# Performer attention with two mixture layers: half tiles of keys of two head pairs in one tile, half tiles of queries of two batches in another, and the low parts of x last in the first layer's sums

## The chip, the cores and the metric

One core of a Trainium2 chip runs the whole program. The metric is the device time of one execution in microseconds (us). The engines are TensorE (PE in the profile; PEld is its load of the stationary operand), VectorE (DVE), ScalarE (ACT), GpSimd (POOL) and SyncE (SP), whose queue issues most DMA transfers.

## The reference

Three layers follow each other. The first is attention with exponential random features, the second a gated feed-forward layer, the third a mixture of eight experts with fixed capacity.

```python
# q, k, v: (4 batches, 8 heads, 576 rows, 64); omega: (128, 64)
def phi(x):
    proj = np.einsum('bhsd,md->bhsm', x, omega)
    h = proj - np.sum(x * x, axis=-1, keepdims=True) / 2.0
    h = h - np.max(h, axis=-1, keepdims=True)
    return np.exp(h) / np.sqrt(m)
q_p, k_p = (phi(q * scale), phi(k * scale))
kv = np.einsum('bhsm,bhsd->bhmd', k_p, v)
z = np.sum(k_p, axis=2)
num = np.einsum('bhsm,bhmd->bhsd', q_p, kv)
den = np.einsum('bhsm,bhm->bhs', q_p, z)[..., None] + 1e-06
# x = num / den as (2304 tokens, 512)
xn = x / rms * rms_g
g = xn @ w_gate
x = (g * sigmoid(g) * (xn @ w_val)) @ w_out          # 512 -> 1536 -> 512
logits = x @ moe2_w_gate                              # greedy: best logits first, 288 tokens per expert
out[mask] = np.maximum(x[mask] @ w1[e], 0.0) @ w2[e]  # for each expert e, 512 -> 1024 -> 512
```

## The kernel before

The attention is cut into **items**, and the items run through a software pipeline of **ticks**: in tick t item t is at lag 0, item t-1 at lag 1, and so on to lag 5. TensorE's order is the order of the code in `run_tick`; the other engines' order is chosen by the scheduler, with the attention at higher priority.

- A **key item** (`KItem(b, p, g)`) is batch b, head pair p, and up to two tiles of 128 keys (g = 0, 1, 2). A batch has 576 keys, four and a half tiles; the fifth is padded with zeros, so the item with g = 2 is short: one tile, half of it padding. At lag 0 a tile and `om` give the features of two heads (`pp`; three matmuls in high and low parts, or one in full precision, L391, for batch 0); VectorE takes the maximum (`mx`, L395), ScalarE the exponentials (`ft`, L398). At lag 1 the features times the values with a column of ones (65 columns a head, L432) are summed in a PSUM tile `pm` over the three items of the pair and copied to `kvs`.
- A **query item** (`QItem(b, t, hf)`) is one tile of 128 queries and four of the eight heads. The tiles of a batch are four whole ones and one of 64 rows, which is computed as a whole one. Lag 0 is as for keys; at lag 1 the features are transposed (L474) and copied (`qp`); at lag 2 they are multiplied with `kvs` (65 columns a head, L478) and VectorE divides (`dn`, L498 to L500); at lags 3 to 5 a tile is normed (`xn`), transposed (L483) and split into `xh` (high part) and `xl` (low part) of a block of 512 tokens.
- A batch has 12 key items and 10 query items, so there are 88 items and 93 ticks. Every float32 product in full precision shows as two records in the trace.
- When a block of 512 tokens is complete, its 24 **feed-forward steps** can run: 12 feature blocks f, for each the gate and the value product (`ffn_pe`, L614 to L616). One step is 12 matmuls of 512 tokens into `gv`, of which there are two; VectorE frees a `gv` with `th` (L626) or `hp` (L634, L638). A tick from `FFN_AT` (25) on holds one step, and a second one as long as weights remain to be converted.
- The weights come as 64-bit numbers. A **conversion** turns half a feature block into float32: ScalarE scales (L542), VectorE joins the words in three instructions (L546 to L548), ScalarE and GpSimd split high and low parts (L570, L571). A tick before `FFN_AT` starts half a conversion, a later one two, until the 24 of the gate and value weights are done. They are loaded to three buffers (`ws`) by SP's queue.

`pm` tiles come from three PSUM buffers, which keys (sums) and queries (transposes, products) share. What is left of the 120 steps when the attention ends runs in a loop behind it; then come the second product with the routing, and the experts.

## Time and profile before

| | |
|---|---|
| time, median of 3 runs | 948.57 us (948.55 to 948.75) |
| profiled execution, its own time | 950.67 us |
| its span | 948.9 us |
| TensorE busy | 924.3 us (97%) |
| VectorE busy | 530.2 us (56%) |
| ScalarE busy | 389.4 us (41%) |
| GpSimd busy | 226.2 us (24%) |
| granted TensorE clock, mean | 0.994 |

Busy time is a sum over stages that have different limits, and TensorE's is modelled at the end of each matmul; so a stage is read from its own stretch, and the price of an instruction of TensorE from the distance between two starts.

### The profile page before, as it was taken

Reading aid. Unit: us, or ns where it says so; the run is one execution under the profiler, and the core shown is the slowest. Engines: PE = TensorE matmul, PEld = TensorE weight load, DVE = VectorE, ACT = ScalarE, POOL = GpSimd, SP = SyncE. Lnnn points to the kernel's source line nnn. Section 1 sums busy time; section 2 is a strip of 40 time slices with the busy share of each in tenths; the row PEclk is TensorE's granted clock in tenths of the full one; section 3 lists DMA queues with packets and bytes.
Section 4 is the critical chain, followed back from the end, with each engine's and each line's share of the span. In section 5 each row is a group of like instructions: output and inputs, shape, how many; then the busy total and the mean of one; then the engine's idle time right before and its main releaser. Section 6 shows DMA issues by size and latency. Waiting matters only on the chain.

```text
span 948.9 us, 16526 instructions
## 1 busy us (share of the span) xinstructions
PE 924.3 (97%) x6349; PEld 804.8 (85%) x6349; DVE 530.2 (56%) x1221; ACT 389.4 (41%) x899; POOL 226.2 (24%) x291
## 2 busy tenths in 40 slices
PE   9998899999999999999999999999999999999996
PEld 7786689988888888877789777777779999999996
DVE  4899946752444334442236476666664655566651
ACT  6976445654554445532234101001004444444451
POOL 1365411322333322443323000000011222222211
PEclk9999999999999999999999999999999999999999
DMA  8546653452222321445666466776632666666650
GB/s 292 178 153 213 210 180 118 152 199 79 78 80 85 104 77 57 167 178 182 207 181 236 140 191 197 221 210 198 189 107 77 192 191 188 211 187 190 188 169 26
DMA packets 117151, 153.67 MB, mean 162 GB/s; under 512 B 6224, under 2 KB 78544, under 8 KB 117072
## 3 DMA queue, kind: packets, MB, share of 16 engines
q1 hardware_dynamic: 111264, 138.32, 46.9%
q0 software_dynamic: 3072, 9.44, 3.3%
q10 hardware_dynamic: 2736, 4.85, 1.3%
q8 instruction: 50, 0.82, 0.4%
q14 instruction: 29, 0.24, 0.1%
HBM read 108.55 MB, written 44.04 MB: 161 GB/s over the span
## 4 chain that ended last, share of the span: by engine, by line
PE 82%; issue 7%; DVE 7%; POOL 1%; DMA 1%; ACT 1%; POOLq 0%; ACTq 0%; SPq 0%; DVEq 0%
PE py L920 15%; PE gv L614 10%; PE gv L616 9%; PE gv L615 9%; PE pm L478 3%; PE ph L1034 3%; PE ph L1031 3%; PE ph L1032 3%; PE pm L432 3%; PE py L1042 3%; PE py L1043 3%; PE py L1044 3%; PE cnt L179 2%; PE pm L474 2%; DVE dw L547 2%
## 5 line engine op out<-in xcount | busy, mean ns | idle before, releaser
L614 PE MATMUL gv<-xh,wc 128*128 128x512 f32 (+1 forms) x480 | 184.9, 385 | 9.1 <-DVE th L626 7.9
L615 PE MATMUL gv<-xl,wc 128*128 128x512 f32 (+1 forms) x480 | 178.3, 371 | 1.5 <-DVE xl L522 1.5
L616 PE MATMUL gv<-xh,wc 128*128 128x512 f32 (+1 forms) x480 | 178.6, 372 | 0.0
L920 PE MATMUL py<-wc,ht 128*128 128x512 f32 x648 | 167.3, 404 | 0.0
L920 PEld LDWEIGHTS py<-wc,ht 128*128 128x128 f32 x648 | 114.8, 189 | 19.0
L614 PEld LDWEIGHTS gv<-xh,wc 128*128 128x128 f32 x480 | 91.4, 190 | 26.6 <-DVE th L626 8.5
L615 PEld LDWEIGHTS gv<-xl,wc 128*128 128x128 f32 x480 | 91.6, 191 | 16.1 <-DVE xl L522 2.2
L616 PEld LDWEIGHTS gv<-xh,wc 128*128 128x128 f32 x480 | 91.1, 190 | 16.4
L398 ACT ACTIVATE ft<-pp,mx 128x128 f32<-128x128 f32 x320 | 92.3, 372 | 18.3 <-DVE mx L395 17.0
L641 POOL TENSOR_TENSOR hp<-th,hp 128x512 fp32r<-128x512 f32 (+1 forms) x48 | 57.8, 1204 | 141.9 <-ACT hp L640 123.9
L626 DVE SCALAR_TENSOR_TENSOR th<-th,gv 128x512 f32<-128x512 f32 (+1 forms) x60 | 37.8, 630 | 94.4 <-ACT th L625 94.3
L891 DVE TENSOR_TENSOR wc<-ws,wc 128x512 fp32r<-128x512 f32 x128 | 84.7, 682 | 0.0
L1042 PE MATMUL py<-ehh,wc 128*128 128x288 f32 x256 | 77.7, 304 | 0.0
L1043 PE MATMUL py<-ehl,wc 128*128 128x288 f32 x256 | 75.9, 297 | 0.0
L1044 PE MATMUL py<-ehh,wc 128*128 128x288 f32 x256 | 75.8, 296 | 0.0
L1031 PE MATMUL ph<-exh,wc 128*128 128x288 f32 x256 | 71.6, 302 | 0.0
L1032 PE MATMUL ph<-exh,wc 128*128 128x288 f32 x256 | 69.8, 295 | 0.0
L931 ACT COPY ys<-py 128x512 f32<-128x512 f32 x18 | 10.6, 588 | 144.2 <-PE py L920 103.3
L901 ACT CAST wc<-ws 128x1024 fp32r<-128x1024 f32 x64 | 66.9, 1046 | 2.4 <-ACT ys L931 2.4
L395 DVE TENSOR_REDUCE mx<-pp 128x4 f32<-128x512 f32 (+1 forms) x88 | 56.0, 636 | 16.7 <-PE pp L388 9.3
L625 ACT ACTIVATE th<-gv 128x512 f32<-128x512 f32 (+1 forms) x60 | 33.3, 555 | 70.4 <-PE gv L616 64.2
L640 ACT CAST hp<-th 128x512 fp32r<-128x512 f32 (+1 forms) x48 | 27.2, 566 | 81.3 <-DVE th L638 80.9
(217 smaller groups left out, 1749.5 us busy)
## 6 DMA issues: line engine op xcount, KB each, us to landing
ws<-in_w_dram SPq DMA_DIRECT2D x64, 512.0 KB, 4.2
ht<-h_dr SPq DMA_DIRECT2D x54, 512.0 KB, 4.2
h_dr<-hp SPq DMA_DIRECT2D x36, 512.0 KB, 3.0
ws<-in_wgv_dram SPq DMA_DIRECT2D x24, 512.0 KB, 4.1
h_dr<-hp SPq DMA_DIRECT2D x24, 256.0 KB, 2.9
ws<-in_wo_dram SPq DMA_DIRECT2D x12, 512.0 KB, 3.9
h_dr<-ht SPq DMA_DIRECT2D x12, 512.0 KB, 3.0
y_dr<-ys ACTq DMA_DIRECT2D x18, 256.0 KB, 4.3
```

The source lines that it names most:

```text
L398: nc.scalar.activation(ft[:n, g], pp[:n, g], AF.Exp, bias=mx[:n, g:g + 1])
L614: nc.tensor.matmul(pg[:, :n], w[:, 0, v, k], xh[:, k, :n], start=(k == 0), stop=False)
L615: nc.tensor.matmul(pg[:, :n], w[:, 0, v, k], xl[:, k, :n], start=False, stop=False)
L616: nc.tensor.matmul(pg[:, :n], w[:, 1, v, k], xh[:, k, :n], start=False, stop=(k == KD - 1))
L891: nc.vector.tensor_sub(w[:, 1, h], sv[:, h], w[:, 0, h])
L901: nc.scalar.copy(w[:, 0], sv)
L920: nc.tensor.matmul(py, ht[:, i4, a], w[:, l, f % 2], start=(f == 0 and n == 0), stop=(f == KF - 1 and n == 2))
L1031: nc.tensor.matmul(ph, w[:, 0, k, m], xh[:, k], start=(k == 0), stop=False)
L1032: nc.tensor.matmul(ph, w[:, 1, k, m], xh[:, k], start=False, stop=False)
L1042: nc.tensor.matmul(py, w[:, 0, k], hh[:, k], start=(k == 0), stop=False)
L1043: nc.tensor.matmul(py, w[:, 0, k], hl[:, k], start=False, stop=False)
L1044: nc.tensor.matmul(py, w[:, 1, k], hh[:, k], start=False, stop=(k == KE - 1))
```

## The change

The half tiles are put together in pairs, on the host and in the kernel:

- **Keys.** The last 64 keys of two head pairs (p = 0, 1 and p = 2, 3) make one tile of 128 (`kC`, loaded by `load_c`). Only odd pairs have an item with g = 2. Its values (`vC`) have 130 columns a head: the first 64 rows are those of one pair, with zeros in the columns of the other, and the other way round. So one product of 130 columns adds to the sums of both pairs, which now stand in one `pm` tile over five items.
- **Queries.** The tokens are cut into 18 tiles of 128 without regard to batches; of the nine tiles of two batches the middle one holds 64 rows of each. It is multiplied with the `kvs` of both batches (130 columns a head, two `pm` tiles, L491 of the kernel after), and `divide` takes each half from its own columns, in eight pieces of 64 rows and a common reciprocal. `kvs` now holds two batches. The middle tile runs with the second batch of the two.
- A batch has 10 key items; the batches have 8, 10, 8 and 10 query items: 76 items and 81 ticks. Block 0 is complete two ticks earlier, and `FFN_AT` is 23.
- Query tiles are split into high and low parts in halves (`kh`, `kl`, 256 columns) instead of whole (`qh`, `ql`, 512); there are two buffers for loaded query tiles instead of one, three for keys and values instead of two.
- In a feed-forward step the four matmuls with `xl` come last.

```diff
-FFN_AT = 25
+FFN_AT = 23
...
+    def load_c(b, r):
...
+            kt = kq.tile([128, 128], F32, name="ktc", bufs=1)
+            vt = kq.tile([128, 2, 2 * (D + 1)], F32, name="vtc", bufs=1)
+        nc.sync.dma_start(kt, kC[b, r])
+        nc.sync.dma_start(vt, vC[b, r])
...
-    def split_q(b, t):
-        qt = qhs[b, t]
-        qh = kq.tile([128, 4, 128], F32R, name="qh")
-        ql = kq.tile([128, 4, 128], F32R, name="ql")
-        nc.vector.tensor_copy(qh, qt)
-        nc.gpsimd.tensor_sub(ql, qt, qh)
+    def split_q(c, hf):
+        src = qhs[c][:, 2 * hf:2 * hf + 2].rearrange("p a t -> p (a t)")
+        qh = kq.tile([128, 256], F32R, name="kh")
+        ql = kq.tile([128, 256], F32R, name="kl")
+        nc.vector.tensor_copy(qh, src)
+        nc.gpsimd.tensor_sub(ql, src, qh)
...
-            self.ts = [t for t in (2 * g, 2 * g + 1) if t < 5]
+            self.ts = (2 * g, 2 * g + 1) if g < 2 else (0,)
...
+                        if g < 2:
+                            nc.tensor.matmul(pk[:, h, o], self.ft[:, 2 * i + h, :], vts[b, p][:, t, h, :],
+                                             start=(first and t == 0 and h == 0), stop=False, skip_group_check=True)
+                        else:
+                            nc.tensor.matmul(pk[:, h].rearrange("p o d -> p (o d)"), self.ft[:, h, :],
+                                             vtc[b, r][:, h, :], start=False, stop=True, skip_group_check=True)
...
+                if self.own is None:
+                    self.pn = [psA.tile([128, 512], F32, name="pm", bufs=3) for _ in range(2)]
+                    for i in range(4):
+                        nc.tensor.matmul(self.pn[i // 2][:, i % 2 * 2 * n:(i % 2 + 1) * 2 * n], self.qp[:, i],
+                                         kv[:, 4 * hf + i].rearrange("p b d -> p (b d)"), start=True, stop=True)
+                    return
...
+            for rows, h, pn in parts:
+                nc.vector.tensor_scalar(dn[rows, h:h + pn.shape[1]], pn[:, :, D], 1e-6 * M, None, op0=OP.add)
+            nc.vector.reciprocal(dn, dn)
+            for rows, h, pn in parts:
+                k, o = pn.shape[1], hf * 256 + h * D
+                nc.vector.tensor_tensor(x[rows, o:o + k * D].rearrange("p (h d) -> p h d", d=D), pn[:, :, :D],
+                                        dn[rows, h:h + k].unsqueeze(2).to_broadcast([pn.shape[0], k, D]), op=OP.mult)
...
         for k in range(KD):
             nc.tensor.matmul(pg[:, :n], w[:, 0, v, k], xh[:, k, :n], start=(k == 0), stop=False)
-            nc.tensor.matmul(pg[:, :n], w[:, 0, v, k], xl[:, k, :n], start=False, stop=False)
-            nc.tensor.matmul(pg[:, :n], w[:, 1, v, k], xh[:, k, :n], start=False, stop=(k == KD - 1))
+            nc.tensor.matmul(pg[:, :n], w[:, 1, v, k], xh[:, k, :n], start=False, stop=False)
+        for k in range(KD):
+            nc.tensor.matmul(pg[:, :n], w[:, 0, v, k], xl[:, k, :n], start=False, stop=(k == KD - 1))
...
-        items += [KItem(b, p, g) for p in range(4) for g in range(3)]
-        items += [QItem(b, t, hf) for t in range(5) for hf in range(2)]
+        items += [KItem(b, p, g) for p in range(4) for g in (range(3) if p % 2 else range(2))]
+        w, o = divmod(b, 2)
+        items += [QItem(w * PAIR + c, hf) for c in range(o * (PAIR // 2), PAIR // 2 + o * (PAIR // 2 + 1))
+                  for hf in range(2)]
```

**TensorE around the first feed-forward step**, in the keys of batch 1. Before, tick 25 (the projections of a full item, then the values of a short item):

```order
L483 MATMUL pm<-cf,xn 128x128 x4
L386 MATMUL pp<-omh,kh 128x256
L387 MATMUL pp<-oml,kh 128x256
L388 MATMUL pp<-omh,kl 128x256
...
L432 MATMUL pm<-vt,ft 128x65 x2
L614 MATMUL gv<-xh,wc 128x512
L615 MATMUL gv<-xl,wc 128x512
L616 MATMUL gv<-xh,wc 128x512
```

Now, tick 23 (the projections of a full item, then the values of a combined item):

```order
L501 MATMUL pm<-cf,xn 128x128 x4
L387 MATMUL pp<-omh,kh 128x256
L388 MATMUL pp<-oml,kh 128x256
L389 MATMUL pp<-omh,kl 128x256
...
L442 MATMUL pm<-vtc,ft 128x130 x2
L642 MATMUL gv<-xh,wc 128x512
L643 MATMUL gv<-xh,wc 128x512
...
L645 MATMUL gv<-xl,wc 128x512 x4
```

The values of a half tile, two products of 65 columns for one head pair, have become two of 130 for two pairs, and the four matmuls with `xl` stand behind the eight with `xh`.

**VectorE around the first feed-forward step** (`dw` is a conversion, `th` and `hp` free a `gv`). Before, 108 instructions stand ahead of the first `th`, eleven whole conversions among them:

```order
L547 SCALAR_TENSOR_TENSOR dw<-ws,dw 128x512 x2
L548 SCALAR_TENSOR_TENSOR dw<-ws,dw 128x512 x2
L546 TENSOR_SCALAR dw<-dw 128x512
L381 CAST qh<-qt 128x512
L547 SCALAR_TENSOR_TENSOR dw<-ws,dw 128x512
L626 SCALAR_TENSOR_TENSOR th<-th,gv 128x512
```

Now, 89 instructions stand ahead of it, nine conversions among them:

```order
L576 SCALAR_TENSOR_TENSOR dw<-ws,dw 128x512
L574 TENSOR_SCALAR dw<-dw 128x512
L575 SCALAR_TENSOR_TENSOR dw<-ws,dw 128x512
L576 SCALAR_TENSOR_TENSOR dw<-ws,dw 128x512
L655 SCALAR_TENSOR_TENSOR th<-th,gv 128x512
```

The cast of a whole query tile is gone from there (its halves follow later), and fewer conversions stand ahead of `th`. From the first to the sixth `th` there are 56 instructions before and 57 now, with 14 and 13 conversions.

**VectorE at the first combined query tile** (tick 30, behind the seventh `th`), now:

```order
L655 SCALAR_TENSOR_TENSOR th<-th,gv 128x512
L514 TENSOR_SCALAR dn<-pm 64x2 x4
L576 SCALAR_TENSOR_TENSOR dw<-ws,dw 128x512
L515 RECIPROCAL dn<-dn 128x4
L574 TENSOR_SCALAR dw<-dw 128x512
L518 TENSOR_TENSOR x<-pm,dn 64x128 x4
```

Where a query item's division was three instructions it is nine here, with pieces of conversions between them.

## Rows read from the trace of the kernel before

**Rows 1.** The chain that ended last, from the page: shares of the span.

```profile
PE 82%; issue 7%; DVE 7%; POOL 1%; DMA 1%; ACT 1%; POOLq 0%; ACTq 0%; SPq 0%; DVEq 0%
```

**Rows 2.** Busy time of each engine in two stretches, in us (instructions in brackets).

```profile
61.30:115.40 54.10, 44.37 (x219) 36.85 (x219) 52.07 (x69) 28.94 (x66) 30.73 (x24) 0.97 0.66 209
...
121.30:529.30 408.00, 407.31 (x2460) 350.51 (x2460) 179.30 (x392) 183.69 (x460) 122.51 (x147) 1.00 0.41 137
```

**Rows 3.** TensorE in order of time: start us, duration us, instruction, idle before it.

```profile
61.33 0.50 PE L614 MATMUL gv<-xh,wc 128*128 128x512 f32 x1 [0.18 <-ACT xh L521]
...
115.37 0.80 PE L614 MATMUL gv<-xh,wc 128*128 128x512 f32 x1 [2.35 <-DVE th L626]
...
121.28 0.48 PE L614 MATMUL gv<-xh,wc 128*128 128x512 f32 x1
...
529.22 0.28 PE L616 MATMUL gv<-xh,wc 128*128 128x256 f32 x1
```

**Rows 4.** VectorE in order of time: casts of query tiles, first and sixth `th`.

```profile
54.61 0.39 DVE L381 CAST qh<-qt 128x512 fp32r<-128x512 f32 x1
...
66.74 1.52 DVE L381 CAST qh<-qt 128x512 fp32r<-128x512 f32 x1
...
68.79 0.67 DVE L626 SCALAR_TENSOR_TENSOR th<-th,gv 128x512 f32<-128x512 f32 x1
...
114.64 0.67 DVE L626 SCALAR_TENSOR_TENSOR th<-th,gv 128x512 f32<-128x512 f32 x1
```

**Rows 5.** GpSimd in order of time, beside the cast at 66.74.

```profile
66.61 1.36 POOL L571 TENSOR_TENSOR wc<-dw,wc 128x512 fp32r<-128x512 f32 x1 [3.08 <-ACT wc L570]
```

**Rows 6.** TensorE in order of time, batch 0 and start of batch 1.

```profile
11.71 1.08 PE L391 MATMUL pp<-wc 128*128 128x256 f32 x4
...
12.63 0.56 PE L432 MATMUL pm<-wc,ft 128*128 128x65 f32 x4
...
46.18 1.08 PE L391 MATMUL pp<-wc,qt 128*128 128x256 f32 x4
...
51.16 0.36 PE L386 MATMUL pp<-omh,kh 128*128 128x256 f32 x1
```

**Rows 7.** TensorE in order of time: a key item, two steps, a query item.

```profile
68.03 0.28 PE L386 MATMUL pp<-omh,kh 128*128 128x256 f32 x1
...
68.74 1.00 PE L432 MATMUL pm<-vt,ft 128*128 128x65 f32 x8
...
69.58 0.60 PE L483 MATMUL pm<-cf,xn 128*128 128x128 f32 x4
...
69.94 0.48 PE L614 MATMUL gv<-xh,wc 128*128 128x512 f32 x1
...
75.52 0.28 PE L386 MATMUL pp<-omh,kh 128*128 128x256 f32 x1
...
138.55 0.36 PE L386 MATMUL pp<-omh,qh 128*128 128x256 f32 x1
...
139.34 0.60 PE L474 MATMUL pm<-cf,ft 128*128 128x128 f32 x4
...
139.77 1.00 PE L478 MATMUL pm<-kvs,qp 128*128 128x65 f32 x8
```

**Rows 8.** Groups by line and form up to 520 us: busy us, mean ns, idle before.

```profile
L615 PE MATMUL gv<-xl,wc 128*128 128x512 f32 x384 | 151.1, 394 | 1.5 <-DVE xl L522 1.5
...
L546 DVE TENSOR_SCALAR dw<-dw 128x512 int32<-128x512 int32 x36 | 20.9, 582 | 3.4 <-ACT dw L542 3.1
...
L547 DVE SCALAR_TENSOR_TENSOR dw<-ws,dw 128x512 int32<-128x512 int32 x36 | 30.5, 852 | 0.5
...
L500 DVE TENSOR_TENSOR x<-pm,dn 128x256 f32<-128x256 f32 x40 | 16.8, 421 | 0.9
...
L382 POOL TENSOR_TENSOR ql<-qt,qh 128x512 fp32r<-128x512 f32 x15 | 19.7, 1311 | 36.4 <-PE pm L474 34.3 <-DVE qh L381 2.1
...
L362 POOL TENSOR_TENSOR kl<-kt,kh 128x256 fp32r<-128x256 f32 x24 | 19.9, 828 | 44.3 <-ACT kh L361 44.3
```

175 lines of the change are left out of this document (91 added, 84 removed).

## Prediction

> **What bounds the kernel now.** I read the chain of waits first [rows 1]: TensorE holds 82% of the chain that ends last, so its work is the price of nearly everything. Where that fails is read from the busy times by stretch [rows 2]. From 121.3 to 529.3 us, TensorE is busy for 407.3 of 408.0 us: whatever matrix work goes away there shortens the span one to one. From 61.3 to 115.4 us it is otherwise: VectorE is busy 52.1 of 54.1 us and TensorE only 44.4, although "busy" flatters it, since ends of matmuls are modelled. The timeline of TensorE [rows 3] shows the switch. The first step of the feed-forward layer starts at 61.33; the 13th, at 115.37, waited 2.35 us for `th`, which VectorE wrote. After that step no such wait is left: the 14th starts at 121.28, and the last matmul of the layer at 529.22. Behind it come 419.7 us (routing, second product, experts), which the diff does not touch.
>
> So there are two terms: when the 14th step starts (a VectorE matter), and how much TensorE work stands behind it.
>
> **TensorE work behind the 14th step.** The pitch of an instruction is the distance from its start to the next one's [rows 7]. A full key item (two tiles) takes 68.03 to 68.74 for the projections and to 69.58 for eight records into `pm`: 0.71 + 0.84 = 1.55 us; a half one 0.78. A query item takes 0.79 (138.55 to 139.34), then 0.43 for four transposes, 0.84 for the products with `kvs` (like those of a key item), and half of the 0.36 that four transposes of `xn` took from 69.58 to 69.94: 2.24 us.
>
> The old 14th step is in tick 32, the new one in tick 30, because the layer starts two ticks earlier (both kernels then run two steps in each of six ticks, and one a tick from there on). Behind it stand, in items still to begin:
> - before: 16 full and 9 short key items, 30 query items;
> - now: 16 full and 4 combined key items, 25 query items.
>
> Five query items fewer: 5 x 2.24 = 11.2 us. Nine short items go: 9 x 0.78 = 7.0. Four combined ones come: half a projection, 0.36, and two products of 130 columns instead of four of 65. No row has such a product. Each is two records in the trace; from below a record cannot beat the 0.105 us of the 65-column one (0.84 / 8), from above it stays under the 0.23 us of a 256-column record in whole numbers (11.71 to 12.63 holds four) [rows 6, 7]. I take 0.117, near the lower end, since the 128-column transposes have a pitch of 0.43 / 4. That gives 0.83 for a combined item, 3.3 in all. In tick 30 the new kernel has started three query items whose later parts are still open, the old one a key item: 2.7 against 0.84, +1.9. Sum: -11.2 - 7.0 + 3.3 + 1.9 = -13.0; the 130 columns of the queries add 0.2. **-12.8 us.** With the upper price for all 64 records of the program it would be 7 us worse.
>
> The reordered sums add and remove nothing on TensorE: twelve matmuls before, twelve after. They can save the waits for the low part, 1.5 us in all [rows 8]. Those of the first block lie in the front, where VectorE sets the pace. I count 0; at best 1.5.
>
> **The start of the 14th step.** Up to the first step, two short key items and two query items of batch 0 leave. A short item of batch 0 costs TensorE half of 0.92 plus half of 0.84; the two items of the fifth query tile lasted from 46.18 to 51.16, 5.0 us [rows 6]. That is 1.8 + 5.0 = 6.8 less. Against it two key items more of batch 1 come first, since the layer now starts in tick 23 and batch 1's keys begin in tick 18: 1.55 us each as pure work, 2.5 with waits. So the first step moves from 61.3 forward by 1.8 to 3.7 us, and VectorE, with 89 instead of 108 instructions ahead of the first `th`, no longer holds it up: I take 3.8, at the upper end of that, for **57.5**.
>
> In the old kernel the first `th` ended at 69.4 [rows 4], 8.1 after its step began: VectorE was in arrears. In the order of the new kernel nine conversions instead of eleven precede it. One conversion is three instructions, 0.58 + 0.85 and a third like the second [rows 8], 2.3 us. So arrears of four to five microseconds fall away and `th` waits for TensorE: step, tanh and `th` itself take about 4.4 us, 61.9 instead of 69.4. From the first to the sixth `th`, VectorE has 56 instructions before and 57 now, of nearly the same kinds (14 conversions before, 13 now). That took 69.4 to 115.2, 45.8 us; so the sixth `th` ends at 107.7 and releases the 13th step. The step (2.8: two of them fill 69.94 to 75.52 [rows 7]) and the attention of tick 30 (0.79 + 0.43 + 0.94 = 2.2) follow: the 14th starts at 112.7 instead of 121.3. **-8.6 us.** That the old 13th step took 5.9 us to the 14th, where its pitch gives 2.8 + 1.6, is in this term: I price the new one at its pitch.
>
> What could take some back:
> - The division of a combined query item is nine VectorE instructions instead of three. The pieces are smaller (64 x 128 instead of 128 x 256); none is free and none costs more than the whole multiplication, 421 ns [rows 8], so six more cost 0 to 2.5 us. I take 1.05 (about 0.18 each). Four items have it; the first two come in ticks 30 and 31, where VectorE is hardly ahead. I charge one of the two, **+1.0**.
> - The low part of a query tile is two GpSimd instructions instead of one: 2 x 828 against 1311 ns [rows 8], 0.35 more. VectorE feels GpSimd: the cast of `qt` took 0.39 us at 54.61, and 1.52 at 66.74, beside a GpSimd subtraction that ran from 66.61 to 67.97 [rows 4, 5]. With two such tiles ahead of the 14th step this is 0 to 0.7 us, inside the range. The Trainium skill (SBUF — State Buffer, "Who interferes with whom") has a lock there: a VectorE cast in its fast mode, or one with two SBUF inputs, waits out a GpSimd instruction. The trace agrees (1.13 us longer); by the rule the sum is 0.7 us less, without it unchanged.
> - Loads: the queries come as one run per partition, keys in more and smaller pieces; a load of weights now stands ahead of the second head pair's keys. No wait of TensorE for keys or queries is on the chain, so 0; if the second pair came late, 2.5 us (a load of 512 KB at the 209 GB/s of [rows 2]).
>
> **Sum:** -12.8 - 8.6 + 1.0 = -20.4 us. The profiled execution took 950.67 us with a span of 948.9, so 930.3 by it; its time is 2.1 above the median of the runs, 948.57, and the same difference gives **928.2 us** for the median.
>
> **The rivals.**
> - *The front stays.* If VectorE reaches the sixth `th` no sooner, because weight loads arrive late for it (SP's queue issues them in order behind loads that wait for free buffers, and there are two more such small buffers with one copy each) or because the 13 conversions fall at a worse moment, the 14th step stays at 121.3 and only the work behind it counts: -12.8 + 1.0, about 936.8. For it: each conversion needs its 512 KB in one of three buffers. Against: VectorE was 96% busy there, so it hardly waited for loads.
> - *All of VectorE's relief counts.* The sixth `th` has 146 instructions ahead of it instead of 164: three conversions (6.8 us) and two query items less, about 10 us. If none of it is lost to waits the step starts up to 3.5 us earlier than I say: about 925.
> - *Slower.* The sums of two head pairs now hold a `pm` buffer for five ticks instead of three, and a combined query item takes two of the three. If TensorE, which works in order, then waits for VectorE's division or ScalarE's copy in every query item, 36 of them eat the 20.4 us from 0.57 us each on, and the kernel is slower: at 1 us each it ends at 964. Little speaks for it: waits of TensorE ahead of these products are too rare in [rows 2] to count (0.7 us of 408), and in a tick 2.7 us of feed-forward work stand between one item's product and the next one's.
> - *No effect.* The halves that went were hidden anyway. Against it stands the busy share after 121 us.
>
> **How the numbers follow.** The forecast has 0.62 (its own range 924 to 932.5), the front that stays 0.17, the full relief 0.11, slower 0.06, no effect 0.04. A change under 0.2% (1.9 us) cannot be told from none. The range leaves out the slower cases and no effect, one in ten, and some 0.08 at its edges: **922.5 to 938**; the upper price of the 130-column product lies in it. Faster 0.90, same 0.04, slower 0.06.
>
> **What would show it.** In the new profile: the first feed-forward matmul at 56 to 59 us, the 13th step at 105 to 110 with or without a wait for `th`, the 14th at 110 to 115, the last near 509; TensorE without gaps between; 130-column products at a pitch of 0.11 to 0.13; no wait for `xl` left; the stages behind still 420 us. The forecast is wrong if waits of 1 us and more stand behind the 14th step (first suspects: the division in ticks 30 to 34, `pm` buffers), if conversions wait for their loads before 110 us, or if the 130-column pitch is near 0.2.

## The result and the profile after

The changed kernel takes 939.69 us (median of 4 runs, 938.03 to 941.22), beside 948.66 for the kernel before on the same chip: a ratio of 0.9901, 95% interval 0.9881 to 0.9921. It is faster, by 9 us and not by the 20.4 of the forecast; 928.2 was forecast, and the time lies 1.7 us above the upper end of the range. The profiled execution took 941.22 us, with a span of 939.4. One execution of e14_at27 (1256.27 us, granted clock 0.654) and one of e16_before_th (1126.23 us, 0.751) are left out of the times and ratios below.

The windows of the kernel after, cut where its 1st, 13th and 18th step begin and where the last matmul of the last step starts (columns: length, then busy time of TensorE, its weight loads, VectorE, ScalarE and GpSimd, then the granted clock, the DMA share and GB/s):

```profile
59.00:109.40 50.40, 44.82 (x219) 37.58 (x218) 49.51 (x67) 28.53 (x64) 25.86 (x21) 0.93 0.68 207
109.40:146.10 36.70, 31.31 (x171) 26.38 (x171) 29.10 (x65) 16.89 (x44) 10.63 (x12) 0.91 0.56 180
146.10:519.80 373.70, 372.76 (x2203) 317.62 (x2202) 172.42 (x364) 158.57 (x387) 116.92 (x146) 1.00 0.40 136
```

The same windows of the kernel before, from its 13th and its 18th step on:

```profile
115.40:140.60 25.20, 25.20 (x148) 22.17 (x148) 13.35 (x26) 12.68 (x34) 3.22 (x4) 0.93 0.65 207
140.60:529.30 388.70, 388.01 (x2339) 333.36 (x2339) 171.12 (x375) 174.18 (x436) 119.97 (x144) 1.00 0.41 135
```

From the 18th step on the new kernel is 15.0 us shorter. The five steps from the 13th to the 18th cost 36.7 us instead of 25.2 and take most of that back; here VectorE is busy for 29.1 us where it was busy for 13.4. What lies behind the last step is 419.6 us (span less the end of the last window), as before.

TensorE in the new kernel in order of time: the 1st, 13th, 14th and 18th step (L642), the waits between them, and the last matmuls of the layer (columns as in [rows 3]):

```profile
59.01 0.50 PE L642 MATMUL gv<-xh,wc 128*128 128x512 f32 x1
...
109.36 0.50 PE L642 MATMUL gv<-xh,wc 128*128 128x512 f32 x1 [1.14 <-DVE th L655]
...
115.17 1.10 PE L485 MATMUL pm<-cf,ft 128*128 128x128 f32 x4 [2.07 <-ACT ft L399]
116.12 1.06 PE L491 MATMUL pm<-kvs,qp 128*128 128x130 f32 x8
116.93 0.47 PE L642 MATMUL gv<-xh,wc 128*128 128x512 f32 x1
...
123.55 1.83 PE L491 MATMUL pm<-kvs,qp 128*128 128x130 f32 x8 [1.51 <-DVE x L518]
...
126.03 0.63 PE L642 MATMUL gv<-xh,wc 128*128 128x512 f32 x1
126.45 0.63 PE L643 MATMUL gv<-xh,wc 128*128 128x512 f32 x1
...
133.11 0.50 PE L642 MATMUL gv<-xh,wc 128*128 128x512 f32 x1 [1.52 <-DVE th L655]
...
146.06 0.48 PE L642 MATMUL gv<-xh,wc 128*128 128x512 f32 x1
...
519.42 0.64 PE L645 MATMUL gv<-xl,wc 128*128 128x256 f32 x4
```

Waits of 1.5 to 2.1 us now stand behind the 13th step, where the kernel before had none (TensorE busy for 25.20 of 25.20 us in the row above): the features of ScalarE come late, behind VectorE's maximum (113.68 to 114.36) and a copy; the products with `kvs` wait for the division's `x`, which still holds a `pm`; the 16th step waits for `th`. The maximum, and behind it ScalarE's copy and features:

```profile
113.68 0.68 DVE L396 TENSOR_REDUCE mx<-pp 128x4 f32<-128x512 f32 x1
```

```profile
114.28 0.57 ACT L527 COPY qp<-pm 128x512 f32<-128x512 f32 x1
114.74 1.15 ACT L399 ACTIVATE ft<-pp,mx 128x128 f32<-128x128 f32 x4
```

Behind the waits of 1.51 and 1.52 us the matmuls start 0.42 us apart (126.03 to 126.45) instead of 0.23: TensorE runs at the lower of its two levels (1.2 instead of 2.4 GHz) for 3 to 4 us after it has stood still, and the granted clock of the stretch is 0.91. Behind the wait of 2.07 us it kept the higher level (1.00 from 109.3 to 121.1 us, in the rows below).

What changed on VectorE is seen from the sixth `th` (which releases the 13th step) to the eighth. First the kernel after, sixth to seventh and seventh to eighth:

```profile
109.30:121.10 11.80, 9.38 (x49) 7.55 (x49) 11.63 (x16) 6.32 (x16) 6.83 (x6) 1.00 0.70 216
121.10:133.10 12.00, 8.97 (x46) 7.41 (x45) 10.80 (x33) 5.65 (x17) 2.79 (x4) 0.86 0.54 173
```

and then the kernel before, likewise:

```profile
115.30:121.30 6.00, 5.93 (x27) 5.05 (x27) 5.27 (x11) 3.17 (x9) 0.68 (x2) 0.72 0.91 284
121.30:130.60 9.30, 9.30 (x60) 8.22 (x59) 2.61 (x7) 3.91 (x10) 1.25 (x2) 1.00 0.60 200
```

In the old kernel VectorE is busy for 7.9 us of 15.3, in the new one for 22.4 of 23.8 (third busy time of each row). It still sets the pace there.

### The profile page after: what moved, and what is told of

Its sections match the earlier page's. It is cut to its first block, busy times and chain, and to the rows that moved or that the text cites. A ratio compares the mean times of both kernels' runs of the same rounds, so it can differ in the third digit from the quotient of the medians.

```text
span 939.4 us, 16221 instructions
## 1 busy us (share of the span) xinstructions
PE 912.3 (97%) x6219; PEld 792.0 (84%) x6219; DVE 536.6 (57%) x1230; ACT 372.5 (40%) x843; POOL 220.8 (24%) x294
## 4 chain that ended last, share of the span: by engine, by line
PE 75%; issue 6%; DVE 2%; POOL 2%; DMA 1%; ACT 0%; SPq 0%; POOLq 0%; ACTq 0%; DVEq 0%
PE py L953 15%; PE gv L642 9%; PE gv L643 9%; PE gv L645 9%; PE ph L1067 3%; PE ph L1064 3%; PE ph L1065 3%; PE py L1075 3%; PE py L1076 3%; PE py L1077 3%; PE pm L496 2%; PE cnt L180 2%; PE pm L439 1%; PE pp L387 1%; PE pm L485 1%
## 5 line engine op out<-in xcount | busy, mean ns | idle before, releaser
L642 PE MATMUL gv<-xh,wc 128*128 128x512 f32 (+1 forms) x480 | 182.1, 386 | 8.0 <-DVE th L655 8.0
L643 PE MATMUL gv<-xh,wc 128*128 128x512 f32 (+1 forms) x480 | 176.4, 374 | 0.0
L645 PE MATMUL gv<-xl,wc 128*128 128x512 f32 (+1 forms) x480 | 120.0, 372 | 0.0
L642 PEld LDWEIGHTS gv<-xh,wc 128*128 128x128 f32 x480 | 91.9, 191 | 27.5 <-DVE th L655 9.4
L645 PEld LDWEIGHTS gv<-xl,wc 128*128 128x128 f32 x480 | 86.5, 191 | 16.1
L399 ACT ACTIVATE ft<-pp,mx 128x128 f32<-128x128 f32 x288 | 82.8, 373 | 26.1 <-DVE mx L396 23.4
L396 DVE TENSOR_REDUCE mx<-pp 128x4 f32<-128x512 f32 (+1 forms) x76 | 49.8, 656 | 15.9 <-PE pp L392 8.4
L669 ACT CAST hp<-th 128x512 fp32r<-128x512 f32 (+1 forms) x48 | 27.1, 565 | 77.7 <-DVE th L667 77.6
```

Source lines behind the costliest of these rows:

```text
L399: nc.scalar.activation(ft[:n, g], pp[:n, g], AF.Exp, bias=mx[:n, g:g + 1])
L642: nc.tensor.matmul(pg[:, :n], w[:, 0, v, k], xh[:, k, :n], start=(k == 0), stop=False)
L643: nc.tensor.matmul(pg[:, :n], w[:, 1, v, k], xh[:, k, :n], start=False, stop=False)
L645: nc.tensor.matmul(pg[:, :n], w[:, 0, v, k], xl[:, k, :n], start=False, stop=(k == KD - 1))
```

## The experiments

Each kernel was timed beside the kernel before on the same chip (which had 948.66 to 950.61 us there, so the ratios are compared rather than the times). The last three columns come from the trace of its profiled execution, from starts read to 0.1 us; the layer's end is the start of its last matmul. Where the doubled ticks begin later (e4_at25, e12_both, e14_at27, e15_27th), four ticks of the attention lie between the 13th and the 18th step instead of five, a query tick of 2.2 us less; there the last column is the one to compare.

| kernel | time, us | ratio to before (95%) | 13th to 18th step, us | 18th step to the layer's end, us | 1st step to the layer's end, us |
|---|---|---|---|---|---|
| before | 948.66 | 1 | 25.2 | 388.6 | 467.9 |
| after | 939.69 | 0.9901 (0.9881 to 0.9921) | 36.7 | 373.7 | 460.8 |
| after_again | 939.87 | 0.9891 (0.9874 to 0.9908) | 36.7 | 374.0 | 461.6 |
| e1_div | 938.43 | 0.9874 (0.9859 to 0.9889) | 36.2 | 374.4 | 460.9 |
| e2_hold | 941.92 | 0.9910 (0.9895 to 0.9925) | 31.6 | 382.1 | 464.3 |
| e3_early | 941.50 | 0.9918 (0.9903 to 0.9932) | 27.9 | 369.7 | 461.4 |
| e4_at25 | 937.11 | 0.9866 (0.9851 to 0.9881) | 28.0 (four ticks) | 374.6 | 456.7 |
| e5_xl_old | 941.91 | 0.9915 (0.9902 to 0.9928) | 36.0 | 373.7 | 463.7 |
| e7_keys | 943.87 | 0.9936 (0.9923 to 0.9949) | 25.5 | 382.9 | 462.8 |
| e8_order | 937.24 | 0.9864 (0.9849 to 0.9878) | 25.2 | 380.8 | 458.3 |
| e9_cast | 938.81 | 0.9883 (0.9865 to 0.9901) | 34.7 | 373.5 | 461.1 |
| e10_warm | 943.53 | 0.9931 (0.9913 to 0.9948) | 31.4 | 373.7 | 463.6 |
| e11_thfirst | 934.89 | 0.9848 (0.9831 to 0.9865) | 32.6 | 373.7 | 457.7 |
| e12_both | 936.97 | 0.9867 (0.9849 to 0.9886) | 21.9 (four ticks) | 384.9 | 459.5 |
| e14_at27 | 933.79 | 0.9830 (0.9817 to 0.9843) | 26.9 (four ticks) | 374.1 | 457.2 |
| e15_27th | 935.07 | 0.9837 (0.9822 to 0.9852) | 27.1 (four ticks) | 373.6 | 455.4 |
| e16_before_th | 949.47 | 0.9994 (0.9985 to 1.0002) | 25.3 | 388.6 | 467.1 |

The theory from the rows above: the conversions now end beside query items, which have much work for VectorE, where they ended beside key items; so VectorE stays the bound for some five steps more. Rivals: the division in nine instructions; the order of the sums; the lower clock by itself.

**The division on whole tiles (e1_div).** The four pieces of 64 rows become two of 128, five instructions instead of nine. It leaves out the 64 rows of the second batch in the four combined items: their columns are divided for the first batch alone.

```diff
-                parts = [(slice(64 * b, 64 * b + 64), 2 * j,
-                          self.pn[j][64 * b:64 * b + 64, :4 * n].rearrange("p (h b d) -> p h b d", h=2, b=2)[:, :, b])
-                         for j in range(2) for b in range(2)]
+                parts = [(slice(0, 128), 2 * j,
+                          self.pn[j][:, :4 * n].rearrange("p (h b d) -> p h b d", h=2, b=2)[:, :, 0])
+                         for j in range(2)]
```

> The changed kernel with the division of the combined query tile done on whole tiles: all 128 rows take the columns of the first batch, so five VectorE instructions instead of nine; the results of the other 64 rows are left out. Theory (the eight pieces of the division, coming while VectorE is saturated, stretch ticks 30 to 33): some 1.0 us less on VectorE in each of the two items there, the 16th step at 130 instead of 133 us, and 2 to 4 us less in all, 936 to 938. Rival (the conversions of the weights are what keeps VectorE saturated there, the division is only in the way): 0 to 1.5 us, 938 to 940. Rival (the order of the sums or PSUM buffers): no difference.

It took 938.43 us; by the ratios that is 1.6 to 2.6 us less than the two measurements of the changed kernel, and the intervals overlap. From the first step to the layer's end it needs 460.9 us (the changed kernel 460.8 and 461.6), from the 13th to the 18th step 36.2. The number of division instructions is not what was lost.

**Holding the conversions of `Wo` (e2_hold)**, which follow those of the gate and value weights in the same tight ticks, until tick 36:

```diff
+HOLD = 36
-        conv_pe(PACE[0] if tick < FFN_AT else PACE[1] if conv["next"] < 2 * KF else PACE[2])
+        conv_pe(PACE[0] if tick < FFN_AT else PACE[1] if conv["next"] < 2 * KF else PACE[2] if tick >= HOLD else 0.0)
```

> The changed kernel, but the conversions of the third weight matrix wait until tick 36 instead of following at once in tick 30. Theory (conversions and query items collide on VectorE in ticks 30 to 34): about two conversions, some 4 to 5 us of VectorE work, leave these ticks; the 18th step starts at 141 to 143 instead of 146 us, the end comes 3 to 6 us earlier, 934 to 937. Rival (the division alone): at most 1 us. A second rival: the conversions come too late later on and feed-forward steps wait for them, slower than 940.

The stretch fell to 31.6 us; 1.6 of the 5.1 us are TensorE's own three `Wo` pieces, which have left it, and the rest says that this work has a part in the stall. But what lies behind the 18th step grew from 373.7 to 382.1, and the time, 941.92, is no better.

**Starting the conversions faster (e3_early)**, more of them a tick before `FFN_AT`:

```diff
-PACE = (0.5, 1.0, 0.5)
+PACE = (0.65, 1.0, 0.5)
```

> The changed kernel with 0.65 instead of 0.5 conversions a tick before the feed-forward layer starts, so 14 or 15 instead of 11 are begun by then. Theory (VectorE idles in the first 50 us and is saturated after 60): three or four conversions, some 7 us, move into the idle time; the two-step ticks end with the keys of batch 1 and the 18th step comes 3 to 6 us earlier, 934 to 937. Rival (loads limit the conversions in the first 30 us, or they delay the attention there): the first step starts later than 59 us and the time stays at 939 to 941.

941.50 us. The surplus reached `Wo` early, and TensorE, in its fixed order, waited 8.6 us for one of its conversions:

```profile
118.27 1.11 PE L613 MATMUL gv<-cf,dw 128*128 128x128 f32 x4 [8.58 <-DVE dw L576]
```

The 13th step began at 122.4 us; here the doubled ticks end one earlier, so that it stands one tick later in the program. So this run does not tell the theories apart. By the first `th` 9.7 conversions had begun to reach VectorE instead of 9.0, though it was busy for only 37.7 of the first 57 us; what held the others back is not shown.

**Doubling later (e4_at25).** The layer still starts in tick 23, with one step and half a conversion a tick until tick 25.

```diff
-FFN_AT = 23
+FFN_AT = 25
```

> The changed kernel with FFN_AT 25 as before. Theory (VectorE is what counts up to tick 33): the start of the first step moves back by two ticks, from 59 to about 63 us, but one conversion more is done by then and VectorE's work is the same, so the 18th step moves by 0 to 3 us and the time is 939 to 943. Rival (the early start is what the change gains): 4 to 6 us slower, 943 to 946.

937.11 us, faster than the changed kernel by 2.4 to 3.3 us by the ratios, at the edge of the intervals. No theory had expected that. It is taken up again below.

**The keys alone (e7_keys).** The queries are those of before.

```diff
-        w, o = divmod(b, 2)
-        items += [QItem(w * PAIR + c, hf) for c in range(o * (PAIR // 2), PAIR // 2 + o * (PAIR // 2 + 1))
-                  for hf in range(2)]
+        items += [QItem(b, t, hf) for t in range(5) for hf in range(2)]
```

> The keys half of the change alone: combined key tiles (ten key items a batch), the order of the sums and FFN_AT 23 as in the changed kernel; queries as before the change (ten items a batch, whole casts, divisions of three instructions). TensorE work saved: about 6 us of the 15. The keys of batch 1 then fill ticks 20 to 29, so the conversions end beside key items, as they did before the change. Theory (conversions that end beside query items keep VectorE the bound): the 13th to the 18th step take 28 us or less, against 36.7 in the changed kernel and 25.2 before, and the time is 940 to 944. Rival (the loss comes with the earlier start of the layer, or with the order of the sums): 33 us or more from the 13th to the 18th step, and 945 to 949.

943.87 us, as the theory said: the keys give all of their 6 us. The stretch from the 13th to the 18th step, with TensorE, VectorE and the clock in the columns as above:

```profile
113.90:139.40 25.50, 25.50 (x150) 22.57 (x150) 21.20 (x38) 14.48 (x36) 8.01 (x7) 0.93 0.71 231
```

There the last conversions of the gate and value weights run beside key items, as before, and 25.5 us are enough, though four of the five ticks hold query items for TensorE. The earlier start of the layer and the order of the sums, which this kernel has too, do not bring the loss. The loss comes with the query half.

**Light items beside the last conversions (e8_order).** Five key items of batch 2 move ahead of the query items of batch 1; `kvs` has two buffers, and loaded keys and values have two instead of three, for room.

```diff
+    items = items[:28] + items[38:43] + items[28:38] + items[43:]
```

> The changed kernel with five key items of batch 2 moved ahead of the ten query items of batch 1 (kvs in two buffers; for their room, the buffers of loaded keys and values are two instead of three). Ticks 28 to 32 then hold light items while the last conversions run; the second block is complete five ticks later. Theory: the 13th to the 18th step fall from 36.7 to 30 us or less, the granted clock over 115 to 150 us rises from 0.90 to 0.95 or more, and the time is 930 to 936. Rival (what is lost there does not depend on the kind of item, or is only put off until the moved items come): 34 us or more there, or waits that come up again up to the 48th step, and 938 to 943.

The stretch fell from 36.7 to 25.2 us:

```profile
110.00:135.20 25.20, 25.20 (x135) 21.85 (x135) 18.33 (x33) 12.46 (x32) 6.83 (x7) 0.88 0.73 228
```

The time, 937.24, is above the forecast of the theory. Of the 11.5 us, 7.1 came back behind the 18th step (380.8 instead of 373.7). Part of that is work put off: five key items, four full ones at 1.55 us and a combined one at some 0.8, were done instead of five query items at 2.24 [rows 7], some 4 us. Part is a hole: a wait of 1.66 us for a `Wo` piece shows there.

```profile
178.89 1.06 PE L617 MATMUL gv<-wg2s,dw 128*128 128x8 f32 x8 [1.66 <-ACT dw L627]
```

So with key items beside the last conversions the stall is gone, as the theory said; the order is a small remedy (by the ratios 2.6 to 3.5 us). One thing more is read from the row: its granted clock is 0.88, lower than the 0.91 of the changed kernel, in a stretch that is 11.5 us shorter. The clock alone is not the loss.

**The cast on ScalarE (e9_cast)**, in `split_q`:

```diff
-        nc.vector.tensor_copy(qh, src)
+        nc.scalar.copy(qh, src)
```

> The changed kernel with the cast of a query tile's half (its high part) on ScalarE instead of VectorE. VectorE loses 28 instructions of 456 ns, 12.8 us in all, of which seven or so (3 us) lie between the 13th and the 18th step. Theory: these 3 us come off the stretch from the 13th to the 18th step, and with fewer stalls the clock stays up: 933 to 937. Rival (ScalarE, which writes the features that TensorE waits for, is as tight as VectorE there, or the stretch is not VectorE's): 938 to 942, with more waits for ft.

938.81 us, the number of the rival: taking 28 casts from VectorE gave nothing that can be told from noise. The stretch is 2 us shorter (at a granted clock of 0.82 in this execution, and with a wait of 3.25 us for `th` ahead of the 16th step), but the 13th step came 2.6 us later, at 112.0. ScalarE and VectorE, in order of time, show a part of the reason:

```profile
105.26 0.66 ACT L570 ACTIVATE dw<-ws 128x512 f32<-128x512 f32 x1 [2.72 <-DMA ws<-in_wgv_dram]
```

```profile
105.95 0.43 DVE L574 TENSOR_SCALAR dw<-dw 128x512 int32<-128x512 int32 x1 [1.74 <-ACT dw L570]
```

VectorE stood idle for 1.74 us for a conversion whose weights had not arrived. In this place less work on VectorE ran into the next limit, the loads of `ws`. In this run the reason that the rival gave (waits for `ft`) did not show.

**Keeping TensorE busy (e10_warm).** In ticks 24 to 33, ahead of the step:

```diff
+        if 24 <= tick < 34:
+            for _ in range(8):
+                nc.tensor.matmul(sink[:, :256], omh[:, :128], omh, start=True, stop=True)
```

> The changed kernel with eight matmuls of 256 columns on constant data, into a bank that nothing reads then, ahead of the first feed-forward step of ticks 24 to 33: 0.91 us a tick, 9.1 us of extra work, of which what falls into a wait costs nothing. Theory that the lower granted clock after each wait costs as much as the waits: the clock over 115 to 150 us rises from 0.90 to 0.95 or more and pays for the work, 936 to 941. Rival (the clock's fall costs little, the waits of VectorE are all): the waits shrink by what the dummies fill, the rest of them is added, 941 to 948.

943.53 us: the clock from 115 to 150 us rose to 0.95, but did not pay for the 9.1 us of extra work; 2.8 to 3.8 were added to the changed kernel's time by the ratios, and the rest fell into waits or was won back by the clock. Which of the two, this run doesn't separate: from the first step to the 13th it took 58.5 us instead of 50.4, more than the extra work there, and the stretch behind is 5.3 us shorter, so other steps stand between 115 and 150 us.

**The release of the banks ahead of the attention's work (e11_thfirst).** The work is the same; the scheduler gives `th` and `hp` the attention's priority.

```diff
-        ffn_step_el()
+        with tc.high_priority(offset=200):
+            ffn_step_el()
```

> The changed kernel with the release of the feed-forward banks (th, hp) at the same priority as the attention, so that VectorE's order has th of the 15th step ahead of the norm xn, a cast and a maximum, where it stands behind them in the changed kernel; the work is the same. Theory that the last of the stalls (from the 15th to the 18th step, 21.1 us against 14.9 before the change) comes from this order while a piece of the Wo conversion holds one of the two banks: the wait of 1.5 us for th ahead of the 16th step goes, with the low clock behind it, and 3 to 5 us of that stretch: 934 to 938. Rival (VectorE has too much work there in any order): the stall moves to the division's x or to another th, 938 to 941.

It took 934.89 us, 4.8 less than the changed kernel (by the ratios 4.1 to 5.0). VectorE ahead of the 16th step, first in the changed kernel:

```profile
128.91 0.43 DVE L574 TENSOR_SCALAR dw<-dw 128x512 int32<-128x512 int32 x1
129.38 0.69 DVE L575 SCALAR_TENSOR_TENSOR dw<-ws,dw 128x512 int32<-128x512 int32 x1
130.78 0.75 DVE L541 SCALAR_TENSOR_TENSOR xn<-x,ss,gr 128x512 f32<-128x512 f32 x1 [0.72 <-POOL ss L538]
131.45 0.29 DVE L382 CAST kh<-qt 128x256 fp32r<-128x256 f32 x1
131.77 0.69 DVE L396 TENSOR_REDUCE mx<-pp 128x4 f32<-128x512 f32 x1
132.38 0.68 DVE L655 SCALAR_TENSOR_TENSOR th<-th,gv 128x512 f32<-128x512 f32 x1
```

and in e11_thfirst:

```profile
126.85 0.69 DVE L575 SCALAR_TENSOR_TENSOR dw<-ws,dw 128x512 int32<-128x512 int32 x1
127.57 0.69 DVE L655 SCALAR_TENSOR_TENSOR th<-th,gv 128x512 f32<-128x512 f32 x1
128.18 0.68 DVE L396 TENSOR_REDUCE mx<-pp 128x4 f32<-128x512 f32 x1
128.78 0.74 DVE L541 SCALAR_TENSOR_TENSOR xn<-x,ss,gr 128x512 f32<-128x512 f32 x1
```

In the changed kernel the norm `xn` of the query tile, which waits for a chain through ScalarE and GpSimd, stands ahead of `th`, with a cast and a maximum behind it; ScalarE had the tanh done at 130.12. At that time a piece of a `Wo` conversion holds one of the two `gv`, so the 16th step waits for the 15th's `th`. Put first, `th` lets the step go after 0.90 us of waiting instead of 1.52. The time came out as the theory said, the place only in part: from the 15th to the 18th step 1.0 us was won (20.0 instead of 21.0), from the 13th to the 15th 3.0, where `th` and the maxima also moved ahead of pieces of conversions. Of the 4.8 us of span, 1.8 are an earlier first step (57.2 instead of 59.0), which other runs show without this edit; 3.1 lie between the first step and the layer's end.

**The two remedies together (e12_both):** the order of items of e8_order, and

```diff
-FFN_AT = 23
+FFN_AT = 25
```

> The order of items of e8_order together with FFN_AT 25 of e4_at25. Theory (both take conversions off VectorE where it is late, by different means, so that the second has less left to win): 13th to 18th step 25 us, 934 to 938. Rival (their gains are of different waits and add): 931 to 934.

936.97 us: the gains don't add. 21.9 us for the five steps (with four ticks of key items beside them), and 384.9 behind them.

**Later still (e14_at27):**

```diff
-FFN_AT = 23
+FFN_AT = 27
```

> FFN_AT 27 instead of 23 in the changed kernel: one feed-forward step and half a conversion a tick up to tick 26, so that the conversions end some two ticks later. If the order of VectorE's work at the 15th to 17th step (th directly behind a division, no xn ahead of it) made the gain of e4_at25, the time here depends on the order that this setting happens to give: 935 to 940, with waits for th where xn stands ahead of it. If a slower start of the conversions is itself the gain, the trend goes on: below 936.

933.79 us, the fastest time here; it, e11_thfirst and e15_27th below are the runs whose intervals lie wholly below both of the changed kernel's. The trend of e4_at25 goes on. That `xn` stands ahead of a `th` costs here as well, a wait of 2.35 us at the 15th step.

These gains do not fit the theory as it stands. When the first query item of batch 1 begins (its first projection, at 99.28 us in the changed kernel), 19.0 conversions have begun on VectorE there, 17.0 in e4_at25 (90.07) and 14.3 here (81.60): more of them stand beside query items in the faster kernels. What differs is seen from the first step to one place of the program, the start of the sixth query item of batch 1: 79.4 us in the changed kernel, 74.2 in e4_at25, with the same 116 instructions of VectorE and the same 16 steps (columns as above):

```profile
59.00:138.40 79.40, 68.43 (x333) 56.80 (x332) 73.66 (x116) 41.00 (x95) 35.38 (x30) 0.91 0.65 200
```

```profile
57.30:131.50 74.20, 62.90 (x325) 52.08 (x324) 72.34 (x116) 40.57 (x94) 34.11 (x30) 0.98 0.70 214
```

TensorE stands idle as long in one as in the other (11.0 and 11.3 us, length less busy time); the granted clock is 0.91 and 0.98. As an estimate, length times what the clock lacks to 1, the lower level costs 7.1 us there and 1.5 here, which is about the difference. (The profiled execution of the changed kernel took 941.22 us against a median of 939.69, that of e4_at25 935.47 against 937.11, so the rows show more than the medians; and one `Wo` piece, 8 matmuls, is missing from the second row.) The other executions say the same: over all of them the mean clock is 0.991 in the changed kernel (ten executions, two runs) and 0.9945 in e4_at25, which makes some 3.5 us of 940, all of its gain; in e14_at27 (0.995) it makes some 4 of 6 us, in e11_thfirst (0.992) 1 of 4 to 5. So starting the doubled ticks later gains mainly by a higher clock, and the order of e11_thfirst mainly by less waiting.

Why less work on VectorE gained nothing (e1_div, e9_cast) is seen before the `hp` of the 16th step, in this order in the changed kernel, e1_div, e9_cast and e4_at25:

```profile
137.72 0.69 DVE L663 SCALAR_TENSOR_TENSOR hp<-gv,th 128x512 f32<-128x512 f32 x1 [3.44 <-PE gv L645]
```

```profile
135.73 0.69 DVE L663 SCALAR_TENSOR_TENSOR hp<-gv,th 128x512 f32<-128x512 f32 x1 [4.84 <-PE gv L645]
```

```profile
138.43 0.69 DVE L663 SCALAR_TENSOR_TENSOR hp<-gv,th 128x512 f32<-128x512 f32 x1 [5.01 <-PE gv L645]
```

```profile
131.28 0.69 DVE L663 SCALAR_TENSOR_TENSOR hp<-gv,th 128x512 f32<-128x512 f32 x1 [0.42 <-PE gv L645]
```

The two engines take turns: TensorE waits for a `th` that stands behind other work of VectorE, and then VectorE, with that work done, waits for TensorE's step. The work taken away came back as a longer idle time of VectorE, 1.4 and 1.6 us longer at this place alone.

**The old order of the sums (e5_xl_old):** the matmul with `xl` stands between those with `xh` again.

```diff
-            nc.tensor.matmul(pg[:, :n], w[:, 1, v, k], xh[:, k, :n], start=False, stop=False)
-        for k in range(KD):
-            nc.tensor.matmul(pg[:, :n], w[:, 0, v, k], xl[:, k, :n], start=False, stop=(k == KD - 1))
+            nc.tensor.matmul(pg[:, :n], w[:, 0, v, k], xl[:, k, :n], start=False, stop=False)
+            nc.tensor.matmul(pg[:, :n], w[:, 1, v, k], xh[:, k, :n], start=False, stop=(k == KD - 1))
```

> The changed kernel with the order of the sums of before (xl between the products of the high parts). Theory: this order has no part in the loss; waits for xl come back, up to 1.5 us: 938 to 941, and the 13th to the 18th step take 35 to 38 us as in the changed kernel. Rival (four matmuls in a row on xl delay the step or the banks): 935 or less.

941.91 us; a wait of 1.04 us for `xl` is back ahead of the second matmul of the first step, and the stretch takes 36.0 us. By the ratios it is 1.3 to 2.3 us slower than the changed kernel, and the intervals overlap. So the new order of the sums is no part of the loss.

**The same priority in the kernel before (e16_before_th)**, at both places of e11_thfirst:

```diff
-        ffn_step_el()
+        with tc.high_priority(offset=200):
+            ffn_step_el()
```

> The kernel before the change with the release of the banks (th, hp) at the priority of the attention, as in e11_thfirst. Theory that the stall of the 15th to 18th step came with the change (xn, cast and maximum of query items ahead of th, where key items stood before): no gain from there, the 13th to the 18th step take 25 us as before, and the time is within 2 us of 949. Rival (th comes late behind conversions in the kernel before, too, and the priority helps any version): 944 to 946.

949.47 us, ratio 0.9994 (0.9985 to 1.0002), and 25.3 us for the stretch. The kernel before has no stall of this kind to cure; the change brought it.

**Priority and a late doubling (e15_27th):** e11_thfirst and

```diff
-FFN_AT = 23
+FFN_AT = 27
```

> The changed kernel with FFN_AT 27 and with the release of the banks at the priority of the attention. Theory (two means against the same waits): 932 to 936, little below either alone. Rival (the gains add, some 4 to 5 us each): 929 to 931.

935.07 us: not below either alone.

**The changed kernel again (after_again).**

> The changed kernel as it is, for the base beside the other two: 938 to 942, and a 13th to 18th step of 34 to 38 us if the stalls come with the order of the instructions, 30 us or less if they were chance of the one profiled execution.

939.87 us, and again 36.7 us from the 13th to the 18th step, with the same waits in the same places. The stall belongs to the order of the program, not to one execution.

## Why the forecast was wrong

**TensorE work behind the 14th step: right.** From the 18th step to the end the new kernel is 15.0 us shorter (373.7 instead of 388.7). Between the 14th and the 18th, its ticks hold query items where the old kernel's are partly key items: 21.7 us of work at the prices of the rows, where the old kernel took 19.3; that leaves 12.6, forecast 12.8. The product of 130 columns, the one price that no row had, lay just below its lower bound of 0.105 us a record: eight records start at 116.12 and the step behind them at 116.93, 0.81 us, as for eight of 65 columns [rows 7]. e7_keys gave the 6 us expected of it.

**The first step: right; the way to the 13th: right by luck.** 57.5 us was forecast for the first step; the executions of kernels with the changed front had 56.9 to 57.7, or 58.8 to 59.3 where the granted clock of the first 25 us was 0.93 (as in the profiled execution of the changed kernel). From the first step to the 13th, 50.4 us passed, forecast 50.2. But the sum holds two errors that cancel. The forecast let VectorE's arrears fall away, so that the first `th` ends 4.4 us after its step began; it ended 7.1 us after (59.01 to 66.08), behind a conversion:

```profile
63.81 1.67 DVE L576 SCALAR_TENSOR_TENSOR dw<-ws,dw 128x512 int32<-128x512 int32 x1
65.40 0.67 DVE L655 SCALAR_TENSOR_TENSOR th<-th,gv 128x512 f32<-128x512 f32 x1
```

ScalarE had the tanh done at 63.86. From there to the end of the sixth `th`, 43.2 us passed instead of the 45.8 taken over from the old kernel. VectorE was in arrears from the first `th` on.

**"The 14th starts at 112.7": here it failed.** The step counts VectorE's work up to the sixth `th`, finds three conversions fewer ahead of it (9 + 13 instead of 11 + 14), and books them as relief; from the 13th step on it prices everything at TensorE's pitch, because the old kernel had no wait for VectorE left behind its 13th step. What the runs showed in its place: VectorE went on setting the pace up to the 18th step. For all conversions have to be done sooner or later, at a fixed pace in ticks, and the new kernel is two ticks earlier in them. The instructions of VectorE, counted in the two orders: ahead of the sixth `th` stood 25.0 conversions and now stand 22.0; 27 of them are done by the seventh `th` before, and only about the eighth now (24.7 ahead of the seventh, 26.7 ahead of the eighth). The three conversions (6.8 us) that the forecast took away from the front of the sixth `th` stand behind it: in the trace, from the sixth to the eighth `th`, VectorE spent 3.4 us on conversions before and 10.4 now (each instruction counted up to the start of the next). Beside them now stand casts (2.8 us; none before), two divisions with their products (3.8) and a norm. Together that is 22.4 us against 7.9, the rows above. The old sixth `th` was the end of VectorE's stretch, the new one is not.

In time: the 14th step began 7.6 us after the 13th instead of the 5.0 forecast. From the 14th to the 18th passed 29.1 us, where four steps of 2.8, four query ticks of 2.2 and three `Wo` pieces (1.6) make some 21.7: 7.4 us too much, with 1.0 charged. The span exceeds the forecast (948.9 less 20.4, 928.5) by 10.9 us: 1.5 from the late first step, 0.1 up to the 13th, 2.6 up to the 14th, 6.4 up to the 18th, and 0.3 behind it.

**What the 36.7 us are made of.** As an estimate from the rows, the work is some 27 us (five steps, five query ticks, three `Wo` pieces). Waits of TensorE behind the 13th step's start make 5.4 (2.07, 0.28, 1.51, 1.52); the clock, 0.91 over 36.7 us, some 3.3 (the kernel before lost 1.8 so in its stretch); some 1 us is not assigned. That the waits came with the query items of the changed kernel beside the doubled conversions is shown: where these conversions end beside key items, the stretch has none (e7_keys and e8_order, 25.5 and 25.2 us). How long the waits are does not go by the number of conversions beside query items (e4_at25 and e14_at27 have more), but by the place of `th`, the maxima and the division's end in VectorE's order (e11_thfirst), nor by VectorE's amount of work alone: with the casts gone (e9_cast) or fewer pieces of division (e1_div), its idle time grew instead. The forecast had no term for the clock. Over all executions it is 0.991 in the changed kernel and 0.9935 in the one before, an estimated 2.5 us of the 11.5 that the median missed by; e4_at25 shows that such a loss can be had back. Which waits bring the lower level and which do not stays open.

**The division, +1.0.** The pieces were dearer than taken, but not what was lost. These groups of the new kernel show it, by line and form (columns as in [rows 8]); the last two are the pieces of e1_div:

```profile
L518 DVE TENSOR_TENSOR x<-pm,dn 128x256 f32<-128x256 f32 x32 | 13.5, 422 | 0.8
...
L382 DVE CAST kh<-qt 128x256 fp32r<-128x256 f32 x28 | 12.8, 456 | 3.2 <-PE pp L388 3.1
...
L518 DVE TENSOR_TENSOR x<-pm,dn 64x128 f32<-64x128 f32 x16 | 4.6, 289 | 0.4
...
L514 DVE TENSOR_SCALAR dn<-pm 64x2 f32<-64x2 f32 x16 | 2.5, 156 | 0.3
```

```profile
L518 DVE TENSOR_TENSOR x<-pm,dn 128x128 f32<-128x128 f32 x8 | 1.9, 282 | 0.1
...
L514 DVE TENSOR_SCALAR dn<-pm 128x2 f32<-128x2 f32 x8 | 1.1, 151 | 0.3 <-PE pm L491 0.3
```

Four pieces of 156 ns and four of 289 in place of 160 and 422 make 1.2 us more an item, where 1.05 was taken. Two such items stand in the stretch, not one; e1_div took four of the six extra instructions of each away, and the stretch shrank by 0.5.

**The low parts in halves, 0 to 0.7.** At the upper end up to the 14th step: four half casts took 2.6 us (1.04, 0.28, 0.28, 1.04), where two whole ones had taken 1.9 before. Behind it the term left something out: a cast of 256 columns takes 0.29 us alone (126.68) and 1.39 beside a GpSimd subtraction (118.49), and the subtraction is one of the weights, not the low part of the query; the mean is 456 ns, so 28 casts cost some 4.7 us more than alone. From the sixth to the seventh `th` two of them took 2.43 us instead of 0.58. VectorE and GpSimd there:

```profile
118.49 1.39 DVE L382 CAST kh<-qt 128x256 fp32r<-128x256 f32 x1
...
126.68 0.29 DVE L382 CAST kh<-qt 128x256 fp32r<-128x256 f32 x1
```

```profile
118.24 1.49 POOL L599 TENSOR_TENSOR wc<-dw,wc 128x512 fp32r<-128x512 f32 x1 [2.01 <-ACT wc L598]
```

The cast ends at 119.88, just behind GpSimd's 119.73. The Trainium skill (SBUF — State Buffer, "Who interferes with whom") states that a VectorE cast in a mode with two ports and a GpSimd instruction lock each other out of the port pair that they share, and that the later one is blocked until the first has ended. The trace agrees: the cast took 1.10 us longer than alone. But more such casts were not the bound by themselves (e9_cast).

**Loads 0 and `xl` last 0.** No wait for keys or queries is listed among TensorE's. The waits for `xl` are gone; with the old order one of 1.04 us comes back (e5_xl_old), so the order of the sums was worth something between the nothing that was counted and the 1.5 us given as its best.

**The rivals.** "The front stays" (936.8) came nearest in time, for another reason: the 14th step did come earlier, 116.9 instead of 121.3, and the time went behind it. "Slower" had the right signs, waits of TensorE for VectorE's division and for `th`, in four ticks and not in all of them. The sign that the prediction had named for being wrong came too: waits of 1 us and more behind the 14th step, 1.51 for the division's `x`, its first suspect, and 1.52 for `th`. "All of VectorE's relief counts" rested on the same mistake as the forecast.

## What to carry to other kernels

When a stage that is bound by one engine starts earlier, look at the point where that engine's whole work is done, not at a landmark of the program such as the sixth of some instruction: work that no longer stands ahead of the landmark stands behind it, and it is priced beside its new neighbours. Count the pieces on the engine's order up to the same amount of work in both kernels, and look what else stands there. The same holds for comparing runs: a stretch between two landmarks is only as long as the work that each kernel has put between them. An instruction that frees a bank for another engine belongs ahead of work with slack, since otherwise the two engines wait in turn and work saved becomes idle time: here that order was worth 0.4 to 0.5%, and nothing in the kernel before. Compare the granted clock of two kernels before anything else: a later start of the doubled conversions was worth 0.6 to 0.7%, most of it by the clock.

## What the hardware showed unexpectedly

- A product of 130 columns took TensorE no longer than one of 65: eight records of either in 0.81 and 0.84 us.
- Half the rows save VectorE nothing: 64 x 128 elements took 289 ns and 128 x 128 took 282 (e1_div); 64 x 2 took 156 ns and 128 x 2 took 151.
- After waits of 1.5 us, matmuls of 512 columns started 0.42 us apart instead of 0.23 for 3 to 4 us; after one of 2.07 us in the same stretch they did not. The mean clock of the stretch still says little about its length (0.88 in 25.2 us, 0.91 in 36.7).
- The first 25 us of the program ran at a granted clock of 1.00 in some executions and 0.93 in others, which moved the first feed-forward step by some 1.7 us.
